# Two MLPs behind linear attention: converted weights kept in DRAM as split parts, and the leaky ReLU moved into ScalarE's pass over the bank

## The chip, the core and the metric

One core of one Trainium2 chip runs the whole program. The time is that of the device for one execution, in microseconds, the median of several runs. TensorE multiplies, VectorE and ScalarE work on tiles element by element, GpSimd does next to nothing here, and SyncE issues all DMA transfers, in order, from one queue.

## The reference

Linear attention with exponential features over 4 batches, 8 heads, 576 tokens of 64 values, then two MLPs over the 2304 tokens of 512 values. The inputs are float64 where the weights are concerned; the result is float32.

```python
def phi(x):
    proj = einsum('bhsd,df->bhsf', x, w_phi)
    proj = proj - max(abs(proj), axis=-1, keepdims=True)
    return concatenate([exp(proj), exp(-proj)], axis=-1)
...
num = einsum('bhsf,bhfd->bhsd', q_p, kv);  den = einsum('bhsf,bhf->bhs', q_p, z)[..., None] + 1e-06
x = num / den                        # [2304, 512]
h = x @ w_in                         # 512 -> 2048
x = maximum(0.01 * h, h) @ w_out     # 2048 -> 512
g = x @ w_gate                       # 512 -> 1536
out = (g / (1 + exp(-g)) * (x @ w_val)) @ w_out2
```

## The kernel before

The program goes batch by batch. The attention of batch 0 runs alone at the start; then come the two MLPs of batch 0, with the attention of batch 1 spread between their units, and so on to the MLPs of the last batch, which run alone.

A *unit* is 24 matmuls: 12 products for each half of the batch's 576 tokens (288 columns), each half in a PSUM bank of its own (`products`, L523 to L533). A hidden tile of 128 features takes one unit in the first MLP (`u_l1`) and two in the second (`u_gate`, `u_val`); 4 hidden tiles are then multiplied by the second weights in 4 units of `u_out`. Each float32 factor is held as a high part in float32r and a low part that is the rest, and a product is made of three matmuls: high by high, high by low, low by high. So a weight tile of 128 x 512 is used as a tile of 128 x 2 x 512, which `w_split` makes: ScalarE copies the high part (L510) and VectorE subtracts it from the whole (`sub`, L57).

The weights come as float64. In batch 0 each tile is loaded as such (`w_load`, L477, 512 KB), turned into float32 by two passes of ScalarE (L491, L492) and three of VectorE (L493 to L499) in `w_to_f32`, and stored as float32 to DRAM (`kept`, L504, 256 KB). Batches 1 to 3 load that copy (L480) and split it again. Eight gate weights are converted in the first attention already (`early`).

The pools hold five buffers for float64 tiles and split tiles of the first weights (`wi`), four for split tiles of the second weights (`wo`), four for float32 weights (`wr`). A tile pool gives a buffer when its last reader is done, so a load can wait for TensorE, VectorE or ScalarE, or for a store. `splits` writes loads ahead by up to five weights, conversions by two. The order on each engine is then laid out once, when the program is built, by a scheduler that goes by priorities and its own estimate of durations; on the chip each engine works through its list in order.

The leaky ReLU stands in `u_l1`. ScalarE copies each half out of its bank into `es` (through `cp`, L60), VectorE then makes max(0.01 g, g) in place over both halves (L554), and `to_parts` splits the result into `gp`:

```python
for c, ps in products(in_ops(("1", b, f), xh, xl, b)):
    cp(g[:, c], ps)
dve.scalar_tensor_tensor(out=g, in0=g, scalar=0.01, in1=g, op0=ALU.mult, op1=ALU.max)
to_parts(g, ("1", b, f))
```

## Time and profile before

| what | value |
|---|---|
| runs | 1099.57, 1102.17 and 1103.4 us, median 1102.17 |
| profiled execution, first to last instruction (span) | 1099.4 us |
| TensorE busy | 1078.7 us (98%), 7728 matmuls |
| VectorE busy | 854.7 us (78%) |
| ScalarE busy | 659.9 us (60%) |
| moved by DMA | 130.25 MB, mean 118 GB/s |

The profile is of one execution; its span lies 2.8 us under the median of the runs. Busy is the time in which at least one instruction of the engine runs. Matmuls are pipelined, so that each lasts about 295 ns while one starts every 133 ns; a gap between two starts shows as idle only as far as it is longer than a matmul lasts.

### The profile page before, as it was taken

How to read it: one execution, taken by the hardware profiler on the slowest of the kernel's cores; microseconds unless marked ns; L12 is line 12 of the kernel's file. 1: busy time of each engine (PE TensorE's matmuls, PEld its weight loads, DVE VectorE, ACT ScalarE, POOL GpSimd, SP SyncE). 2: the span in 40 equal slices, each digit the busy share in tenths (PEclk: the TensorE clock that was granted, in tenths of full speed). 3: DMA queues.
4: the chain of work that ended last, by engine and by line, in shares of the span. 5: the costliest groups of instructions: out<-in, count | busy, mean ns of one | idle time of the engine just before them, and what ended most of it. 6: DMA issues, size and time to landing. Idle time of an engine off the chain costs nothing.

```text
span 1099.4 us, 20402 instructions
## 1 busy us (share of the span) xinstructions
PE 1078.7 (98%) x7728; PEld 1041.9 (95%) x7728; DVE 854.7 (78%) x1765; ACT 659.9 (60%) x1457; POOL 6.8 (1%) x28
## 2 busy tenths in 40 slices
PE   7899999999999999999999999999999999999998
PEld 6668999999998999999999999999999999999998
DVE  6998889898999888779778888878787645565553
ACT  7768877667766787556646576655563444344421
POOL 1000000000000000000000000000000000000000
PEclk9999999999999999999999999999999999999999
DMA  9735766454654532223223322232131232323211
GB/s 332 237 93 174 213 209 194 154 155 155 211 185 125 172 100 91 80 57 110 62 76 108 103 73 89 77 98 97 36 97 51 80 99 77 92 82 106 97 48 44
DMA packets 69329, 130.25 MB, mean 118 GB/s; under 512 B 17136, under 2 KB 17392, under 8 KB 69232
## 3 DMA queue, kind: packets, MB, share of 16 engines
q1 hardware_dynamic: 69232, 128.95, 37.8%
q8 instruction: 61, 1.00, 0.4%
q14 instruction: 36, 0.29, 0.1%
HBM read 106.38 MB, written 22.54 MB: 117 GB/s over the span
## 4 chain that ended last, share of the span: by engine, by line
PE 82%; DVE 5%; DMA 5%; ACT 5%; issue 1%; SPq 0%; ACTq 0%; DVEq 0%
PE pm L530 70%; PE pa L391 4%; DMA wi<-in_w_dram 3%; PE pa L200 3%; PE pa L159 2%; DVE wr L499 1%; DMA wi<-in_wv_dram 1%; DVE wr L494 1%; ACT wr L491 1%; PE pm L299 1%; PE pa L344 1%; ACT wi L492 1%; PE pa L365 1%; PE pa L334 0%; PE pa L335 0%
## 5 line engine op out<-in xcount | busy, mean ns | idle before, releaser
L530 PE MATMUL pm<-xh,wi 128*128 128x288 f32 x2560 | 534.0, 297 | 2.2 <-ACT wi L510 1.6
L530 PEld LDWEIGHTS pm<-xh,wi 128*128 128x128 f32 x2560 | 416.5, 188 | 6.1 <-ACT wi L510 1.8
L530 PE MATMUL pm<-gp,wo 128*128 128x288 f32 x2688 | 385.3, 296 | 2.6 <-ACT acc L60 1.5
L530 PE MATMUL pm<-xl,wi 128*128 128x288 f32 x1280 | 378.9, 297 | 0.0
L530 PEld LDWEIGHTS pm<-gp,wo 128*128 128x128 f32 x2688 | 365.3, 188 | 6.6 <-ACT acc L60 1.8
L530 PEld LDWEIGHTS pm<-xl,wi 128*128 128x128 f32 x1280 | 240.4, 188 | 2.5 <-issue 1.7
L510 ACT ACTIVATE wi<-wr 128x512 fp32r<-128x512 f32 x160 | 101.0, 635 | 59.9 <-PE pm L530 34.6
L57 DVE TENSOR_TENSOR wi<-wr,wi 128x512 fp32r<-128x512 f32 x160 | 108.9, 682 | 14.2 <-ACT wi L510 13.0
L588 DVE TENSOR_TENSOR acc<-pm,acc 128x288 f32<-128x288 f32 x160 | 70.8, 453 | 57.1 <-PE pm L530 56.2
L510 ACT ACTIVATE wo<-wr 128x512 fp32r<-128x512 f32 x112 | 67.2, 630 | 65.5 <-PE pm L530 59.5
L57 DVE TENSOR_TENSOR wo<-wr,wo 128x512 fp32r<-128x512 f32 x112 | 74.3, 682 | 31.0 <-ACT wo L510 30.8
L57 DVE TENSOR_TENSOR gp<-es,gp 128x576 fp32r<-128x576 f32 x112 | 83.8, 749 | 13.5 <-ACT gp L60 12.6
L60 ACT ACTIVATE gp<-es 128x576 fp32r<-128x576 f32 x112 | 76.7, 687 | 25.0 <-DVE es L554 15.6
L561 ACT ACTIVATE es<-pm 128x288 f32<-128x288 f32 x96 | 39.4, 413 | 45.1 <-PE pm L530 44.5
L60 ACT ACTIVATE es<-pm 128x288 f32<-128x288 f32 x128 | 52.5, 417 | 16.5 <-PE pm L530 16.0
L57 DVE TENSOR_TENSOR fl<-ff,fh 128x512 fp32r<-128x512 f32 (+1 forms) x72 | 51.0, 714 | 13.0 <-ACT fh L60 12.7
L569 DVE SCALAR_TENSOR_TENSOR es<-pm,es 128x288 f32<-128x288 f32 x96 | 43.0, 450 | 23.0 <-PE pm L530 22.7
L492 ACT ACTIVATE wi<-wi 128x512 int32<-128x512 uint32 x60 | 41.2, 687 | 32.7 <-DMA wi<-in_w_dram 20.2
L562 DVE SCALAR_TENSOR_TENSOR es<-es,pm 128x288 f32<-128x288 f32 x96 | 42.1, 444 | 20.5 <-ACT es L561 19.9
L554 DVE SCALAR_TENSOR_TENSOR es<-es 128x576 f32<-128x576 f32 x64 | 48.0, 751 | 8.7 <-ACT es L60 8.7
L491 ACT ACTIVATE wr<-wi 128x512 f32<-128x512 f32 x60 | 40.7, 684 | 15.8 <-DMA wi<-in_w_dram 4.7
L394 ACT ACTIVATE dn<-pa 64x288 f32<-64x288 f32 x64 | 26.1, 408 | 37.8 <-PE pa L391 36.8
(108 smaller groups left out, 1282.1 us busy)
## 6 DMA issues: line engine op xcount, KB each, us to landing
wr<-kept SPq DMA_DIRECT2D x212, 256.0 KB, 2.8
wi<-in_w_dram SPq DMA_DIRECT2D x44, 512.0 KB, 4.3
kept<-wr SPq DMA_DIRECT2D x68, 256.0 KB, 4.1
wi<-in_wv_dram SPq DMA_DIRECT2D x12, 512.0 KB, 4.1
raw<-in_kT_dram SPq DMA_DIRECT2D x16, 288.0 KB, 3.1
raw<-in_qT_dram SPq DMA_DIRECT2D x16, 288.0 KB, 3.1
out_dram<-acc SPq DMA_DIRECT2D x16, 288.0 KB, 2.4
gp<-in_wg_dram SPq DMA_DIRECT2D x8, 512.0 KB, 7.8
```

The lines of the kernel that those rows point to most:

```text
L57: dve.tensor_tensor(out=o, in0=a, in1=b, op=ALU.subtract)
L60: act.activation(o, a, AF.Copy)
L391: pe.matmul(ps, w, x, start=(i == 0), stop=(i == len(ops) - 1))
L491: act.activation(t, high.bitcast(F32), AF.Abs, scale=REBIAS)
L492: act.activation(low, low.bitcast(U32), AF.Copy, scale=2.0**-29)
L510: i = act.activation(t[:, 0], r, AF.Copy)
L530: m = pe.matmul(ps, w, x[:, c], start=(i == 0), stop=(i == n - 1))
L554: dve.scalar_tensor_tensor(out=g, in0=g, scalar=0.01, in1=g, op0=ALU.mult, op1=ALU.max)
L561: act.activation(t[:, c], ps, AF.Tanh, scale=0.5)
L562: dve.scalar_tensor_tensor(out=t[:, c], in0=t[:, c], scalar=1.0, in1=ps, op0=ALU.add, op1=ALU.mult)
L569: dve.scalar_tensor_tensor(out=g[:, c], in0=ps, scalar=0.5, in1=g[:, c], op0=ALU.mult, op1=ALU.mult)
L588: dve.tensor_tensor(out=acc[o][:, t], in0=ps, in1=acc[o][:, t], op=ALU.add)
```

## The change

Weights are split once. `w_split` now ends by storing both parts to DRAM in one transfer of 512 KB, and batches 1 to 3 load the parts straight into the tile that TensorE reads. The store of the float32 form goes, but for the eight gate weights of `early`, which keep it (`ready`). `wo` has five buffers in place of four, `wr` three in place of four. In `u_l1` ScalarE makes the leaky ReLU (Prelu with slope 0.01) as it empties the bank, and VectorE's pass goes. That each half has a bank of its own is so before as well.

```diff
-    kept = {}
+    kept, ready = {}, {}
+    def parts_tile(key):
+        wtile[key] = t = T([P, 2, 512], F32R, *(("wo", 5) if key[0] in "23" else ("wi", 5)))
+        return t
+    def flat(t):
+        return t.rearrange("p a n -> p (a n)").bitcast(F32)
+    def keep(cols, src_ap):
+        uid[0] += 1
+        d = dram.tile([P, cols], F32, name=f"kept_{uid[0]}")
+        nc.sync.dma_start(out=d, in_=src_ap)
+        return d
     def w_load(key, tag="wi", n=5):
-        kind, b, f = key
-        if b == 0 and (kind, f) not in kept:
+        kind, _, f = key
+        if (kind, f) in kept:
+            nc.sync.dma_start(out=flat(parts_tile(key)), in_=kept[kind, f])
+        elif (kind, f) in ready:
+            wf[key] = t = T([P, 512], F32, "wr", 3)
+            nc.sync.dma_start(out=t, in_=ready[kind, f])
+        else:
             w64[key] = t = T([P, 512, 2], I32, tag, n)
             nc.sync.dma_start(out=t.rearrange("p n t -> p (n t)"), in_=src[kind][f].bitcast(I32))
-        else:
-            wf[key] = t = T([P, 512], F32, "wr", 4)
-            nc.sync.dma_start(out=t, in_=kept[kind, f])
 ...
-        t = T([P, 512], F32, "wr", 4)
+        t = T([P, 512], F32, "wr", 3)
 ...
         wf[key] = t
-        kind, _, f = key
-        uid[0] += 1
-        kept[kind, f] = d = dram.tile([P, 512], F32, name=f"kept_{uid[0]}")
-        nc.sync.dma_start(out=d, in_=t)
     def w_split(key):
-        kind, b, f = key
+        if key not in wf:
+            return
         r = wf.pop(key)
-        wtile[key] = t = T([P, 2, 512], F32R, *(("wo", 4) if kind in "23" else ("wi", 5)))
+        t = parts_tile(key)
         i = act.activation(t[:, 0], r, AF.Copy)
         tc.stamp_issue_order_token(i.ins, "weights")
         sub(t[:, 1], r, t[:, 0].bitcast(F32))
+        kept[key[0], key[2]] = keep(1024, flat(t))
     def early(key):
         w_load(key, "gp", 5)
         w_to_f32(key)
-        del wf[key]
+        ready[key[0], key[2]] = keep(512, wf.pop(key))
 ...
         for c, ps in products(in_ops(("1", b, f), xh, xl, b)):
-            cp(g[:, c], ps)
-        dve.scalar_tensor_tensor(out=g, in0=g, scalar=0.01, in1=g, op0=ALU.mult, op1=ALU.max)
+            act.activation(g[:, c], ps, AF.Prelu, alpha=0.01)
         to_parts(g, ("1", b, f))
```

The scheduler lays out the whole list anew. The first place is ScalarE's list around the first unit of batch 0. L510 (now L523) is the copy of a weight's high part; `wi_68_294` (now `wi_66_290`) is the fourth weight of the first MLP and `wo_284_945` (now `wo_282_940`) the first of its second product; `es` is the output of a unit. Before:

```order
L492 ACTIVATE wi_65_284<-wi_65_284 128x512 [waits DMAHW2_49]
L510 ACTIVATE wi_68_294<-wr_62_273 128x512 [waits DVE_49,Activation_49]
L510 ACTIVATE wo_284_945<-wr_66_286 128x512
L394 ACTIVATE dn_227_758<-pa_226_755 64x288 [waits PE_49]
L394 ACTIVATE dn_227_758<-pa_231_770 64x288 [waits PE_49]
L491 ACTIVATE wr_298_1007<-wi_65_284 128x512 [waits DVE_49]
L60 ACTIVATE xh_222_745<-xf_221_742 128x288 [waits DVE_49]
L373 ACTIVATE ff_252_831<-pa_251_828 128x288 [waits PE_49]
```

And of the change:

```order
L508 ACTIVATE wi_64_282<-wi_64_282 128x512 [waits DMAHW2_49,Activation_49]
L170 ACTIVATE ff_332_1148<-pa_330_1144,mn_333_1149 128x128 [waits DVE_49,PE_49,Activation_49]
L171 ACTIVATE ff_332_1148<-pa_330_1144,mk_331_1146 128x128
L170 ACTIVATE ff_332_1148<-pa_330_1144,mn_333_1149 128x128
L171 ACTIVATE ff_332_1148<-pa_330_1144,mk_331_1146 128x128
L523 ACTIVATE wi_66_290<-wr_61_271 128x512 [waits PE_49]
L567 ACTIVATE es_277_902<-pm_279_917 128x288
L523 ACTIVATE wo_282_940<-wr_65_284 128x512
L170 ACTIVATE ff_340_1193<-pa_338_1189,mn_341_1194 128x128 [waits DVE_49,Activation_49]
L171 ACTIVATE ff_340_1193<-pa_338_1189,mk_339_1191 128x128
L567 ACTIVATE es_293_971<-pm_295_986 128x288 [waits PE_49]
```

Before, both copies stand among the last steps of the first attention (L394, L373), ahead of every unit's output; now they stand among the keys of the next attention (L170, L171) and the outputs of the first units (L567), and the first of them waits for TensorE.

The second place is VectorE's list a little later, at the outputs of the first units: L554 is the leaky ReLU, L57 with `wi`, `wo` or `gp` a subtraction that makes a low part, L164 and L168 belong to the next attention. Before:

```order
L554 SCALAR_TENSOR_TENSOR es_278_904<-es_278_904 128x576 [waits Activation_49]
L57 TENSOR_TENSOR wi_288_958<-wr_282_937,wi_288_958 128x512 [waits PE_49,Activation_49]
L57 TENSOR_TENSOR wo_300_1015<-wr_286_950,wo_300_1015 128x512 [waits Activation_49]
L57 TENSOR_TENSOR wo_312_1072<-wr_298_1007,wo_312_1072 128x512 [waits Activation_49]
L164 TENSOR_REDUCE mk_351_1253<-pa_350_1251 128x2 [waits PE_49]
L57 TENSOR_TENSOR wo_329_1143<-wr_310_1064,wo_329_1143 128x512 [waits Activation_49]
L554 SCALAR_TENSOR_TENSOR es_294_974<-es_294_974 128x576 [waits Activation_49]
L554 SCALAR_TENSOR_TENSOR es_306_1031<-es_306_1031 128x576 [waits Activation_49]
```

And of the change:

```order
L57 TENSOR_TENSOR wi_66_290<-wr_61_271,wi_66_290 128x512 [waits Activation_49]
L57 TENSOR_TENSOR wo_282_940<-wr_65_284,wo_282_940 128x512 [waits Activation_49]
L164 TENSOR_REDUCE mk_350_1246<-pa_349_1244 128x2 [waits PE_49]
L168 TENSOR_SCALAR mn_352_1249<-mk_350_1246 128x2 [waits DVE_49]
L164 TENSOR_REDUCE mk_361_1301<-pa_360_1299 128x2 [waits PE_49,Activation_49]
L168 TENSOR_SCALAR mn_363_1304<-mk_361_1301 128x2 [waits DVE_49]
L57 TENSOR_TENSOR gp_280_931<-es_277_902,gp_280_931 128x576 [waits Activation_49]
L509 TENSOR_SCALAR wr_285_947<-wr_285_947 128x512 [waits Activation_49]
L509 TENSOR_SCALAR wr_297_1003<-wr_297_1003 128x512 [waits Activation_49]
```

The three passes of L554 are gone. Where the low parts of the fifth weight and of the second, third and fourth `wo` tile stood, now the fourth weight and the first `wo` tile are made, and conversions (L509) stand behind them.

The third place is SyncE's list in the second batch, where kept weights are loaded. Before:

```order
L480 DMA wr_1365_6413<-kept_710_3046 128x512 [waits DMAHW4_49,DVE_49]
L480 DMA wr_1381_6483<-kept_729_3147 128x512 [waits DMAHW6_49,DVE_49]
L480 DMA wr_1383_6488<-kept_230_768 128x512 [waits DMAHW7_49,DVE_49]
L480 DMA wr_1388_6524<-kept_754_3282 128x512 [waits DMAHW0_49,DVE_49]
L480 DMA wr_1405_6596<-kept_243_806 128x512 [waits DMAHW5_49,DMAHW1_49,DVE_49]
```

And of the change:

```order
L490 DMA wi_1012_4603<-kept_358_1293 128x1024 [waits DMAHW2_49,PE_49]
L490 DMA wi_1023_4659<-kept_369_1348 128x1024 [waits DMAHW3_49,PE_49]
L490 DMA wi_1049_4778<-kept_390_1430 128x1024 [waits DMAHW4_49,PE_49]
L490 DMA wi_1098_5028<-kept_452_1724 128x1024 [waits DMAHW5_49,PE_49]
L130 DMA raw_1324_6209<-in_qT_dram 128x576 [waits DMAHW6_49,DVE_49]
L490 DMA wo_1064_4864<-kept_404_1495 128x1024 [waits DMAHW7_49,PE_49]
```

A load waited for VectorE, which had to split the tile that was in its `wr` buffer; now it waits for TensorE, which has to be done with the tile in its `wi` or `wo` buffer.

## Rows read from the trace of the kernel before

**Rows 1.** The page: span, and busy time of each engine with its instructions

```profile
span 1099.4 us, 20402 instructions
PE 1078.7 (98%) x7728; PEld 1041.9 (95%) x7728; DVE 854.7 (78%) x1765; ACT 659.9 (60%) x1457; POOL 6.8 (1%) x28
```

**Rows 2.** By stages: us, busy PE, PEld, DVE, ACT, POOL (instructions), clock, DMA share, GB/s

```profile
0.00:87.00 87.00, 74.83 (x328) 57.59 (x328) 73.40 (x187) 62.44 (x144) 4.88 (x21) 1.00 0.67 220
87.00:220.00 133.00, 131.66 (x903) 126.02 (x904) 116.75 (x239) 104.59 (x249) 1.87 (x7) 1.00 0.61 188
220.00:345.00 125.00, 121.25 (x852) 115.23 (x851) 116.27 (x254) 84.69 (x173) 0.00 (x0) 1.00 0.56 176
345.00:603.00 258.00, 257.98 (x1939) 254.03 (x1938) 213.42 (x441) 166.32 (x385) 0.00 (x0) 1.00 0.31 94
603.00:860.00 257.00, 257.00 (x1937) 253.49 (x1935) 210.69 (x425) 154.39 (x332) 0.00 (x0) 1.00 0.27 80
860.00:1099.40 239.40, 235.94 (x1778) 235.54 (x1776) 124.12 (x223) 87.44 (x176) 0.00 (x0) 1.00 0.26 80
```

**Rows 3.** The chain that ended last, its last long piece: start us, us, what

```profile
862.81 233.15 PE pm L530 x1756
```

**Rows 4.** Waits of PE, 87 to 345 us: us in total, times, longest

```profile
PE pm L530 <- ACT wi L510: 1.6, 1, 1.6
PE pm L530 <- ACT acc L60: 1.5, 1, 1.5
```

**Rows 5.** The timeline, 258 to 264 us: start, us, engine, instruction, idle before

```profile
261.25 0.67 ACT L492 ACTIVATE wi<-wi 128x512 int32<-128x512 uint32 x1 [0.70 <-DMA wi<-in_wv_dram]
...
262.41 1.85 PE L530 MATMUL pm<-gp,wo 128*128 128x288 f32 x12 [1.51 <-ACT acc L60]
```

**Rows 6.** Waits of ScalarE for float64 loads, 87 to 345 us

```profile
ACT wi L492 <- DMA wi<-in_w_dram: 20.2, 15, 2.6
ACT wi L492 <- DMA wi<-in_wv_dram: 10.5, 8, 2.0
```

**Rows 7.** Groups by line: busy us, mean ns of one, idle before and its releasers

```profile
L57 DVE TENSOR_TENSOR wi<-wr,wi 128x512 fp32r<-128x512 f32 x160 | 108.9, 682 | 14.2 <-ACT wi L510 13.0
L510 ACT ACTIVATE wi<-wr 128x512 fp32r<-128x512 f32 x160 | 101.0, 635 | 59.9 <-PE pm L530 34.6 <-DMA wr<-kept 11.3 <-issue 10.2
...
L57 DVE TENSOR_TENSOR wo<-wr,wo 128x512 fp32r<-128x512 f32 x112 | 74.3, 682 | 31.0 <-ACT wo L510 30.8
...
L510 ACT ACTIVATE wo<-wr 128x512 fp32r<-128x512 f32 x112 | 67.2, 630 | 65.5 <-PE pm L530 59.5 <-DMA wr<-kept 4.4 <-DVE wr L499 1.4
L60 ACT ACTIVATE es<-pm 128x288 f32<-128x288 f32 x128 | 52.5, 417 | 16.5 <-PE pm L530 16.0
...
L554 DVE SCALAR_TENSOR_TENSOR es<-es 128x576 f32<-128x576 f32 x64 | 48.0, 751 | 8.7 <-ACT es L60 8.7
...
L561 ACT ACTIVATE es<-pm 128x288 f32<-128x288 f32 x96 | 39.4, 413 | 45.1 <-PE pm L530 44.5
...
L175 ACT ACT_TABLE_LOAD x1 | 1.3, 1283 | 0.7 <-PEq L758 0.7
```

**Rows 8.** Line L554 alone, 87 to 220 us: us, VectorE busy (instructions)

```profile
87.00:220.00 133.00, 11.93 (x16) 1.00 0.61 188
```

**Rows 9.** DMA: queue 1, and transfers with KB each and median us to landing

```profile
q1 hardware_dynamic: 69232, 128.95, 37.8%
...
wr<-kept SPq DMA_DIRECT2D x212, 256.0 KB, 2.8
wi<-in_w_dram SPq DMA_DIRECT2D x44, 512.0 KB, 4.3
kept<-wr SPq DMA_DIRECT2D x68, 256.0 KB, 4.1
```

**Rows 10.** Groups by line: conversions of weights

```profile
L499 DVE TENSOR_TENSOR wr<-wr,wi 128x512 uint16<-128x512 uint16 x60 | 44.8, 751 | 0.2
...
L492 ACT ACTIVATE wi<-wi 128x512 int32<-128x512 uint32 x60 | 41.2, 687 | 32.7 <-DMA wi<-in_w_dram 20.2 <-DMA wi<-in_wv_dram 10.5 <-DMA wi<-in_wg_dram 1.7
```

## The prediction

> **What bounds the kernel now.** I read the busy times first: TensorE is busy 1078.7 of 1099.4 us, VectorE 854.7, ScalarE 659.9 [rows 1]. With an engine at 98%, what other engines save can only shorten the 20.7 us in which it is not busy, so the next view is the one by stages, where the reader is to see where these lie [rows 2]. The columns give: 12.2 us idle before 87 us (first attention, start-up loads), 1.3 from 87 to 220 (first batch, first MLP), 3.8 from 220 to 345 (first batch, second MLP), 0.02 from 345 to 860 (the second and third batch), and 3.5 behind 860 us, most of it the last result's way out. The chain of waits ends in one piece of 1756 matmuls in 233.15 us [rows 3]: 132.8 ns each. In the last three batches TensorE runs at that pace without a gap that this view shows, and VectorE (83% from 345 to 860 us) and ScalarE (60 to 64%) keep ahead of it. The granted clock is 1.00, the higher level of 2.4 GHz, in every stage [rows 2], so no term stands for it.
>
> So the reader should look at the first batch, 87 to 345 us, alone. There all weights are converted from float64, and VectorE is at 88 and 93% [rows 2]. The waits of TensorE in that stretch name two large ones: 1.6 us for a weight copy by ScalarE and 1.5 us for an evacuation into acc by ScalarE [rows 4]. In both cases ScalarE was late for the same reason: its queue is in order, and a conversion that waits for a float64 tile stands in front. The row at 261.25 us shows it: the conversion had waited 0.70 us for its load, and behind it comes the evacuation that TensorE waits 1.51 us for [rows 5]. ScalarE waits for such loads 20.2 + 10.5 us in this stretch [rows 6].
>
> **The change part by part.**
>
> *Splits in the later batches.* 204 weight tiles (68 in each of three batches) are no longer split: ScalarE loses 204 x 0.63 = 129 us, VectorE 204 x 0.68 = 139 us [rows 7]. All of it lies beside matmuls, in stages whose TensorE idle time is 0.02 us. Gain on the path: 0, since this view leaves 0.02 us to win there. The two splits of a tile also leave the way of a weight from its load to its use, which makes the later batches safer, not faster.
>
> *Leaky ReLU.* The copy out of the bank costs 417 ns, the Tanh with the same shape 413 [rows 7]: on this engine the function does not set the price, so I take 417 for Prelu (bounds 413 and, were it two passes, 834: 128 x 417 = 53 us more of ScalarE over the run, hidden except in 87 to 220 us, where 32 of them are 13 us). VectorE loses 64 passes of 0.75 us, 48 us; 11.93 us of that in 87 to 220 us [rows 7, 8]. The Trainium skill's page ScalarE: Activation LUTs, section Rules for kernel authors, says to put relu and max on VectorE rather than ScalarE. By that rule the move would be a loss. The row says otherwise here, because the ScalarE pass over the bank is there already: 417 ns stay 417 ns, and 751 ns go. What the move can win is the 1.3 us of TensorE idle time in 87 to 220 us [rows 2], from a VectorE queue that is shorter by 9% there. I take 1.3.
>
> *Second MLP of the first batch.* No leaky ReLU lies here, and the conversions and splits of this batch's own weights stay. Only the splits for the next batch's first tiles go at its end. The 3.8 us come from ScalarE waiting for loads, which is not removed. I take a gain of 0.5 (0 to 2).
>
> *Loads and stores.* A reload was 256 KB and landed in 2.8 us; it becomes 512 KB, for which the float64 loads of the same size say 4.3 us [rows 9]. 204 x 0.262 MB = 53 MB more are read; 68 stores double and 8 early ones are added, 76 x 0.262 = 20 MB more. Queue 1 moved 128.95 MB in 37.8% of the engines' time [rows 9], so 202 MB are about 59% (an estimate in proportion). In the later batches 94 GB/s become about 163 at a share of 0.31, so about 0.54: room remains, and the buffers are asked for several units ahead. The first batch is tighter: its share is 0.61 and 0.56 at 188 and 176 GB/s [rows 2]; 20 MB over 258 us are 77 GB/s more, a share near 0.83. A float64 load then takes longer than 4.3 us, and ScalarE's queue stands for that time. Price: from 0 (it hides under the lead of the loads) to the 23 waits for loads [rows 6] being 0.5 us longer each, of which two large ones reach TensorE now and four may: +2. I take +0.5.
>
> *Order in the first batch.* This is the part the diff does not tell. The program as built splits the fourth weight of the first MLP behind a wait for TensorE, where before it was done ahead of the first unit; the first weight of the second product comes behind it too. A split is 0.63 us on ScalarE and then 0.68 on VectorE [rows 7], which are ten matmuls at 132.8 ns. Counted in the built order, eleven of the first batch's 68 weights now have their last split step released by a matmul that lies under 15 places ahead of their first use; before there were two. One converted buffer fewer (wr 4 to 3) and split tiles that are held for their store make this lead shorter. Where the lead is shorter than the split, TensorE waits for the rest: 0 to 1.3 us each, up to the 1.6 us of the one case that the trace has [rows 4]. Some of the eleven lie next to each other and share one wait, and the low part is asked for a few matmuls behind the high one, so I take four waits of 0.5: +2. Bounds 0 and six times 1.6.
>
> *Start-up.* Before the first unit's output ScalarE has seven instructions fewer (conversions at 0.69 and copies at 0.63 us), and VectorE the passes that belong to them, the longest 0.75 us [rows 7, 10]. The 12.2 us before 87 us are mostly first loads; I take a gain of 1.2 (0 to 3).
>
> **The sum.** -1.3 - 0.5 + 0.5 + 2 - 1.2 = -0.5 us on the profiled 1099.4 us: 1098.9. The runs have a median of 1102.17, 2.8 us above that span, so the time is about 1101.7 us.
>
> **The rivals.** *Gaps close (faster).* The freed VectorE time lets conversions run ahead, and all 5.1 us of 87 to 345 us go, with some 2 us of the start: 1102.2 - 7 = 1095 us. For it: VectorE at 88 and 93% is the fullest engine behind TensorE there. Against it: the two largest waits are ScalarE's, and behind loads.
>
> *Weights late in the first batch (slower).* The place is the first group of the second product and the second MLP's weights in the first batch: splits released by the matmuls just before. Six such waits of 1 to 1.6 us are +6 to +10, with nothing won: 1108 us. It decides from four waits on. For it: the shorter leads, the fuller DMA queue. Against it: the list was ordered with these leads known, and the units in between can fill.
>
> *Reloads late in the later batches (slower).* The 512 KB come too late after all. 204 loads with 0.1 us of wait each are 20 us: 1122 us. Against it: loads are released four or more units, over 12 us, ahead.
>
> *Table loads (slower).* Prelu would need another table than Exp and Tanh, which stand between the units. One load is 1.28 us [rows 7]; two for each of 64 units are 164 us, 41 of them in 87 to 220 us, where ScalarE has 28 us free: at least 13 us, 1115 us. The built program has a single table load, as before, so this has next to no chance. The same page (section Table sets) lists relu, copy and abs as in every set, but not Prelu by name, and no run here shows it yet.
>
> **How the numbers follow.** Little changes: 0.42, 1101.7 us, own range 1098 to 1106. Gaps close: 0.30, 1092 to 1098. Weights late: 0.25, 1106 to 1112. Reloads late 0.02, tables 0.01. What a measurement of this kernel can tell from no change is about 0.3%, 3.3 us, so 1098.9 to 1105.5 counts as the same. Faster 0.30, same 0.42, slower 0.28. The range 1092 to 1111 leaves out the two small rivals and the ends of the others, 2 in 10 at most.
>
> **What would show it.** Right: TensorE's idle time stays between 15 and 22 us, all of it before 345 us; the later batches keep their 258 and 257 us; Prelu takes 0.41 to 0.43 us; VectorE is near 667 us, ScalarE near 531, 204 MB are moved. Wrong on the first batch: TensorE waits for copies into wi or wo of over 6 us in 87 to 345 us (slower), or none of over 1 us and ScalarE's waits for loads under 20 us (faster). Wrong on the later batches: waits of TensorE for kept tiles. Wrong on the start: the first unit begins more than 3 us earlier or later.

## The result, and the profile after

The changed kernel takes 1114.53 us (median of 4 runs, 1112.89 to 1115.18) beside 1102.5 us for the kernel before: ratio 1.011, 95% interval 1.0095 to 1.0125. That is 12 us slower, and 3.5 us above the range of the prediction.

The page shows the work gone as forecast, and TensorE, which has the same 7728 matmuls, busy for longer and idle for longer than in [rows 1]: 28.7 us of the span against 20.7.

```profile
span 1113.3 us, 19800 instructions
PE 1084.6 (97%) x7728; PEld 1046.2 (94%) x7728; DVE 705.0 (63%) x1497; ACT 561.5 (50%) x1253; POOL 6.7 (1%) x28
...
q1 hardware_dynamic: 70384, 202.35, 52.6%
...
L567 ACT ACTIVATE es<-pm 128x288 f32<-128x288 f32 x128 | 52.9, 416 | 107.5 <-PE pm L544 107.0
...
wi<-kept SPq DMA_DIRECT2D x120, 512.0 KB, 3.3
wo<-kept SPq DMA_DIRECT2D x84, 512.0 KB, 5.2
wi<-in_w_dram SPq DMA_DIRECT2D x44, 512.0 KB, 5.1
kept<-wi SPq DMA_DIRECT2D x40, 512.0 KB, 4.2
```

Prelu out of the bank (L567) takes 416 ns where the copy took 417 [rows 7]; a reload of parts lands in 3.3 to 5.2 us, a float64 load in 5.1 in place of 4.3 [rows 9]. VectorE has 150 us less to do and ScalarE 98, and none of it came back as time.

The view by stages answers [rows 2], with the same columns and bounds:

```profile
0.00:87.00 87.00, 76.24 (x324) 59.88 (x324) 68.15 (x173) 57.78 (x136) 4.75 (x21) 0.96 0.60 199
87.00:220.00 133.00, 129.28 (x870) 121.39 (x871) 108.54 (x225) 105.44 (x249) 1.92 (x7) 1.00 0.74 256
220.00:345.00 125.00, 116.90 (x805) 110.71 (x805) 114.06 (x245) 81.98 (x167) 0.00 (x0) 0.99 0.69 234
345.00:603.00 258.00, 255.37 (x1916) 250.99 (x1915) 170.46 (x364) 136.36 (x321) 0.00 (x0) 1.00 0.50 175
603.00:860.00 257.00, 257.00 (x1937) 253.67 (x1937) 165.46 (x342) 122.41 (x266) 0.00 (x0) 1.00 0.42 148
860.00:1113.30 253.30, 249.83 (x1884) 249.56 (x1882) 78.32 (x151) 57.56 (x116) 0.00 (x0) 1.00 0.45 158
```

The reader should look at two columns. TensorE's count of matmuls is 4 lower ahead of 87 us, 33 lower from 87 to 220, 47 lower from 220 to 345 and 23 lower from 345 to 603 us: 107 in all, about 14.2 us at 132.8 ns each, of work that had to follow later; the span is 13.9 us longer. The last 23 are lost by 380 us (the lines below, from 87 to 380 us, before and then after, differ by 105; a matmul across the edge of two windows counts in both), so the loss lies in the first batch and where it passes into the second. The granted clock, 1.00 everywhere before, is 0.96 ahead of 87 us and 0.99 from 220 to 345 us. From 380 us on TensorE is busy up to the last result's way out (3.5 us idle behind 860 us, as before): the loads of 512 KB harm nothing there.

```profile
87.00:380.00 293.00, 287.89 (x2017) 275.79 (x2018) 265.81 (x561) 215.86 (x489) 1.87 (x7) 1.00 0.58 179
```

```profile
87.00:380.00 293.00, 278.55 (x1912) 263.42 (x1913) 254.58 (x540) 211.88 (x477) 1.92 (x7) 0.99 0.72 250
```

What TensorE waits for from 220 to 380 us is neither the weights of [rows 4] nor the accumulator. It is steps of the next batch's attention (L334, L365, L391):

```profile
PE pa L334 <- ACT ff L374: 4.0, 2, 3.4
PE pa L365 <- DVE mrow L354: 2.4, 1, 2.4
PE pa L391 <- DVE xf L409: 1.8, 1, 1.8
PE pm L544 <- DVE es L575: 1.1, 1, 1.1
PE pm L544 <- DVE wi L57: 0.7, 1, 0.7
PE pa L200 <- DVE fl L57: 0.4, 1, 0.4
PE pm L544 <- ACT wi L523: 0.3, 1, 0.3
```

The largest of them in the timeline (start, us, engine, instruction, idle before):

```profile
304.06 0.29 PE L544 MATMUL pm<-xl,wi 128*128 128x288 f32 x1
...
305.87 0.67 ACT L508 ACTIVATE wi<-wi 128x512 int32<-128x512 uint32 x1 [2.07 <-DMA wi<-in_w_dram]
...
306.55 0.41 ACT L394 ACTIVATE dn<-pa 64x288 f32<-64x288 f32 x1
306.97 0.41 ACT L373 ACTIVATE ff<-pa 128x288 f32<-128x288 f32 x1
...
307.27 0.40 ACT L374 ACTIVATE ff<-pa 128x288 f32<-128x288 f32 x1
...
307.73 0.40 PE L334 MATMUL pa<-pk,wst_h 128*128 128x288 f32 x1 [3.37 <-ACT ff L374]
```

ScalarE stands 2.07 us at a conversion whose float64 tile has not landed; three attention steps stand behind it in its queue; TensorE waits 3.37 us for the last of them. This is the shape of [rows 5], with an attention step in the place of the accumulator. Ahead of the two next largest waits ScalarE has stood in the same way, and steps of VectorE stand between it and TensorE:

```profile
243.87 0.70 ACT L508 ACTIVATE wi<-wi 128x512 int32<-128x512 uint32 x1 [1.43 <-DMA wi<-in_wv_dram]
...
246.75 0.53 PE L365 MATMUL pa<-mrow,sel 128*128 128x288 f32 x2 [2.38 <-DVE mrow L354]
...
321.85 0.67 ACT L508 ACTIVATE wi<-wi 128x512 int32<-128x512 uint32 x1 [2.57 <-DMA wi<-in_wg_dram]
...
324.27 1.94 PE L391 MATMUL pa<-ff,kvh 128*128 128x288 f32 x7 [1.77 <-DVE xf L409]
```

The first attention looks worse too. Windows of ten us there, before, then after:

```profile
20.00:30.00 10.00, 9.52 (x47) 8.09 (x45) 8.02 (x19) 9.90 (x26) 1.03 (x4) 1.00 1.08 387
30.00:40.00 10.00, 9.10 (x40) 6.51 (x39) 9.83 (x25) 9.07 (x22) 0.98 (x3) 1.00 0.85 253
```

```profile
20.00:30.00 10.00, 8.13 (x38) 6.20 (x37) 8.42 (x19) 9.91 (x25) 1.04 (x4) 0.98 1.07 387
30.00:40.00 10.00, 9.82 (x32) 7.86 (x33) 8.00 (x20) 6.66 (x16) 0.63 (x2) 0.68 0.76 240
```

and what stands there in the timeline after:

```profile
26.52 0.67 ACT L507 ACTIVATE wr<-wi 128x512 f32<-128x512 f32 x1
...
27.08 0.67 ACT L508 ACTIVATE wi<-wi 128x512 int32<-128x512 uint32 x1
...
27.64 0.42 ACT L176 ACTIVATE ff<-ff 128x256 f32<-128x256 f32 x1
...
27.94 0.63 ACT L523 ACTIVATE wi<-wr 128x512 fp32r<-128x512 f32 x1
...
28.15 1.10 PE L200 MATMUL pa<-ff,pk 96*128 96x256 f32 x4 [1.13 <-issue]
...
28.46 0.68 ACT L508 ACTIVATE wi<-wi 128x512 int32<-128x512 uint32 x1
...
29.03 0.42 ACT L175 ACTIVATE ff<-ff 128x256 f32<-128x256 f32 x1
...
29.48 0.42 ACT L176 ACTIVATE ff<-ff 128x256 f32<-128x256 f32 x1
...
29.95 2.08 PE L200 MATMUL pa<-ff,pk 96*128 96x256 f32 x4 [0.69 <-ACT ff L176]
...
31.82 3.62 PE L159 MATMUL pm<-wbd,raw 128*128 128x256 f32 x8
```

Conversions and splits of the first MLP's weights (L507, L508, L523) stand ahead of the attention's L175 and L176. TensorE stands idle for 1.13 us (till just behind the end of an L176), then for 0.69 us; before, the same two gaps were 0.48 and 0.18 us. Behind that the granted clock is 0.68 from 30 to 40 us, a mean between the two levels of 2.4 and 1.2 GHz, and 32 matmuls start there in place of 40.

Yet little of it is left a few steps later. By 70 us both kernels have started 249 matmuls, the first unit begins at 68.20 us where it began at 67.77, and by 87 us the count is 324 against 328, about 0.5 us. So the crowded start is plain to see and is not where the 12 us went.

### The profile page after: what moved, and what is told of

Read it like the earlier page. It is cut to its first block, busy times and chain, and to the rows that moved or that the text cites. A ratio compares the mean times of both kernels' runs of the same rounds, so it can differ in the third digit from the quotient of the medians.

```text
span 1113.3 us, 19800 instructions
## 1 busy us (share of the span) xinstructions
PE 1084.6 (97%) x7728; PEld 1046.2 (94%) x7728; DVE 705.0 (63%) x1497; ACT 561.5 (50%) x1253; POOL 6.7 (1%) x28
## 3 DMA queue, kind: packets, MB, share of 16 engines
q1 hardware_dynamic: 70384, 202.35, 52.6%
## 4 chain that ended last, share of the span: by engine, by line
PE 86%; DMA 5%; ACT 4%; DVE 3%; issue 1%; SPq 0%; ACTq 0%; DVEq 0%
PE pm L544 73%; PE pa L391 4%; PE pa L200 4%; DMA wi<-in_w_dram 3%; PE pa L159 2%; DMA wi<-in_wv_dram 1%; PE pm L299 1%; ACT wi L508 1%; DMA kept<-wi 1%; PE pa L334 1%; PE pa L344 1%; PE pa L238 1%; PE pa L365 1%; PE pa L335 1%; DVE wr L515 0%
## 5 line engine op out<-in xcount | busy, mean ns | idle before, releaser
L544 PE MATMUL pm<-gp,wo 128*128 128x288 f32 x2688 | 390.0, 296 | 0.2 <-DVE acc L601 0.2
L57 DVE TENSOR_TENSOR gp<-es,gp 128x576 fp32r<-128x576 f32 x112 | 84.4, 754 | 98.8 <-ACT gp L60 98.4
L567 ACT ACTIVATE es<-pm 128x288 f32<-128x288 f32 x128 | 52.9, 416 | 107.5 <-PE pm L544 107.0
L57 DVE TENSOR_TENSOR fl<-ff,fh 128x512 fp32r<-128x512 f32 (+1 forms) x72 | 51.4, 716 | 18.5 <-ACT fh L60 17.5
L508 ACT ACTIVATE wi<-wi 128x512 int32<-128x512 uint32 x60 | 41.2, 687 | 28.5 <-DMA wi<-in_w_dram 17.2
L200 PE MATMUL pa<-ff,pk 128*128 128x256 f32 (+1 forms) x160 | 44.5, 395 | 4.4 <-issue 3.4
L60 ACT ACTIVATE fh<-ff 128x512 fp32r<-128x512 f32 (+1 forms) x72 | 47.6, 664 | 0.9
L394 ACT ACTIVATE dn<-pa 64x288 f32<-64x288 f32 x64 | 26.1, 407 | 40.8 <-PE pa L391 39.7
L515 DVE TENSOR_TENSOR wr<-wr,wi 128x512 uint16<-128x512 uint16 x60 | 44.6, 751 | 0.6
L507 ACT ACTIVATE wr<-wi 128x512 f32<-128x512 f32 x60 | 39.8, 683 | 8.2 <-DMA wi<-in_w_dram 3.8
L60 ACT ACTIVATE acc<-pm 128x288 f32<-128x288 f32 x64 | 26.1, 422 | 33.4 <-PE pm L544 33.0
L510 DVE SCALAR_TENSOR_TENSOR wr<-wi,wr 128x512 int32<-128x512 int32 x60 | 40.9, 686 | 0.8
```

The source lines that it names most:

```text
L57: dve.tensor_tensor(out=o, in0=a, in1=b, op=ALU.subtract)
L60: act.activation(o, a, AF.Copy)
L200: pe.matmul(ps[:, 256 * h : 256 * h + 256], v[:n, h].rearrange("p a d -> p (a d)"), part[b, j, s][:n, h].rearrange("p a f -> p (a f)"), st ...
L508: act.activation(low, low.bitcast(U32), AF.Copy, scale=2.0**-29)
L510: dve.scalar_tensor_tensor(out=ti, in0=high, scalar=-0x80000000, in1=ti, op0=ALU.bitwise_and, op1=ALU.bitwise_or)
L515: dve.tensor_tensor(out=t16, in0=t16, in1=e16, op=ALU.add)
```

## The experiments

Three theories: **the ring** (three buffers for converted weights in place of four), **the stores** (512 KB of parts for each weight in the first batch, which also hold the split tile), **the order** (any edit makes the scheduler draw a new order, and this one is bad). The price of the order can't be removed, only drawn again. Ratios are to the kernel before on the same chip, with their 95% intervals; the kernel before has medians of 1101.65 to 1103.04 us on these chips, so a difference of two times from different chips is good to about 1.4 us.

**Each half of the change alone.** The first edit is the leaky ReLU alone, the second the stored parts alone:

```diff
--- before.py, Prelu alone
-            cp(g[:, c], ps)
-        dve.scalar_tensor_tensor(out=g, in0=g, scalar=0.01, in1=g, op0=ALU.mult, op1=ALU.max)
+            act.activation(g[:, c], ps, AF.Prelu, alpha=0.01)
--- after.py, parts alone
-            act.activation(g[:, c], ps, AF.Prelu, alpha=0.01)
+            cp(g[:, c], ps)
+        dve.scalar_tensor_tensor(out=g, in0=g, scalar=0.01, in1=g, op0=ALU.mult, op1=ALU.max)
```

> The kernel before with the leaky ReLU alone moved to ScalarE (Prelu); weights are stored as float32 and split in every batch as before. If what was lost comes from the smaller ring of converted weights (theory one) or from the doubled stores and the tiles that they hold (theory two), neither is here: 1098 to 1103 us, no clock row under 0.95 and no wait of TensorE over 2.5 us between 87 and 380 us. If it comes from any new order that the list scheduler makes, whatever the edit (theory three), the time can lie anywhere from 1095 to 1112 us.

> The changed kernel with the leaky ReLU put back: a Copy out of the bank by ScalarE, then a pass over both halves by VectorE. Theories one and two: the loss stays, 1112 to 1118 us, waits of TensorE for attention steps (the lines 334, 365, 391) between 220 and 345 us of over 5 us in all. Theory three: anywhere from 1098 to 1118 us. If Prelu itself were the harm, 1099 to 1103 us.

Measured: Prelu alone 1102.72 us, 1.0002 (0.9992 to 1.0013): no change. Parts alone 1118.91 us, 1.0159 (1.0134 to 1.0185). The loss belongs to the stored parts and the rings that were set with them. That parts alone is 4.4 us slower than the whole change says nothing of Prelu: a redraw, below, moves as much. And the mark that I gave did not come: TensorE does not wait for attention steps there but for weights, as these largest waits from 87 to 380 us show (L200 belongs to the attention):

```profile
PE pm L544 <- ACT wi L523: 9.2, 7, 2.5
PE pa L200 <- issue: 2.3, 3, 1.8
PE pm L544 <- DVE wi L57: 1.8, 2, 1.6
PE pm L544 <- ACT wo L523: 1.1, 1, 1.1
```

**Four buffers, a single store, and both.**

```diff
--- after.py, four buffers
-            wf[key] = t = T([P, 512], F32, "wr", 3)
+            wf[key] = t = T([P, 512], F32, "wr", 4)
...
-        t = T([P, 512], F32, "wr", 3)
+        t = T([P, 512], F32, "wr", 4)
--- after.py, a single store
-        kept[key[0], key[2]] = keep(1024, flat(t))
+        if not kept:
+            one.append(keep(1024, flat(t)))
+        kept[key[0], key[2]] = one[0]
```

> The changed kernel with four buffers for converted weights again in place of three; nothing else. Theory one (the ring of three): ScalarE's waits for a converted buffer to come free (on the subtraction of line 57) go, and the time falls to 1099 to 1105 us. Theory two (stores): 1111 to 1116 us. Theory three: some other time between 1098 and 1118 us, and the waits lie in other places.

> The changed kernel with a single store: the parts of the first split weight are stored, and all later batches load these same 512 KB in place of their own weight, so the later batches compute with a wrong weight; what is left out is 67 of the 68 stores of parts (35 MB) and the wait of a tile for its store. Theory two: 1098 to 1104 us, the DMA share from 87 to 345 us falls from 0.72 to near 0.5, and float64 loads land in about 4.3 us in place of 5.1. Theory one: 1111 to 1116 us. Theory three: any other time between 1098 and 1118 us.

> The changed kernel with a single store of parts (later batches load these 512 KB in place of their own weight and so compute with a wrong one) and four buffers for converted weights. Each of the two alone left most of the loss (1113.8 and 1111.2 us). If the smaller ring and the stores do the harm together, each able to do it alone, this is 1098 to 1104 us. If the new order of the instructions does it, the time stays over 1106 us, with waits of TensorE for attention steps between 220 and 380 us, although neither the ring nor the stores are left to blame.

Measured: four buffers 1111.15 us, 1.0082 (1.0065 to 1.0099); a single store 1113.76, 1.0105 (1.0089 to 1.0122); both 1101.8, 0.9993 (0.9982 to 1.0003). With three buffers the stores cost nothing that can be told (1114.53 against 1113.76), although the DMA share from 87 to 380 us falls from 0.72 to 0.42 without them: the bytes are not the cause there. The windows, first of four buffers, then of four buffers and a single store, show what the ring does from 87 to 380 us; the changed kernel has 278.55 us and 1912 matmuls there.

```profile
30.00:40.00 10.00, 8.77 (x25) 6.93 (x26) 8.41 (x20) 6.14 (x15) 0.63 (x2) 0.66 0.94 276
87.00:380.00 293.00, 287.27 (x1972) 273.78 (x1971) 248.23 (x529) 208.75 (x472) 1.88 (x7) 0.99 0.71 247
```

```profile
30.00:40.00 10.00, 8.74 (x27) 6.95 (x28) 8.81 (x22) 6.50 (x16) 0.63 (x2) 0.68 0.67 197
87.00:380.00 293.00, 289.56 (x2030) 277.81 (x2029) 250.45 (x536) 211.12 (x482) 1.88 (x7) 1.00 0.45 143
```

The fourth buffer gives TensorE 9 us and 60 matmuls in that stretch, yet the time falls by 3.4 us only: the start is worse in this kernel than in the changed one, TensorE is busy for 40.3 us from 40 to 87 us in place of 43.5, and 297 matmuls start ahead of 87 us in place of 324. The clock row from 30 to 40 us is low in both lines, 0.66 and 0.68, and the second kernel takes no longer than the kernel before: a low row there is not by itself a loss. One mark of the ring theory failed: ScalarE's waits at L507 for VectorE to free a buffer (L57) did not go (3.7 us from 87 to 380 us with three buffers, 1.9 + 1.8 by its two rows, and 3.1 with four).

**An extra buffer in the kernel before, and both kernels under another scheduler.**

```diff
--- before.py
-        wtile[key] = t = T([P, 2, 512], F32R, *(("wo", 4) if kind in "23" else ("wi", 5)))
+        wtile[key] = t = T([P, 2, 512], F32R, *(("wo", 5) if kind in "23" else ("wi", 5)))
--- before.py and after.py
-    with _tile.TileContext(nc, schedule_with_timeline_sim=True) as tc:
+    with _tile.TileContext(nc, schedule_with_timeline_sim=False) as tc:
```

> The kernel before with one more buffer for the split weights of the second products (five in place of four), and nothing else: more room, no work. If the loss is physical (ring, stores, transfers), this is 1097 to 1103 us. If the order that the scheduler makes decides, a changed ring gives another order, and the time can lie anywhere from 1095 to 1115 us.

> The kernel before, with its instructions ordered by priority alone in place of by the scheduler's own model of time. It serves as the other half of the next run: a second pair of before and after under another order. The time itself is open, 1100 to 1250 us.

> The changed kernel, ordered by priority alone as in the run ahead of it. If the harm is physical (shorter ring, stores that hold tiles), it is slower than that run by 8 us or more. If the harm is one draw of the scheduler, the difference of the two has no reason to be of that sign: between -15 and +15 us, and faster if the work that VectorE and ScalarE lose counts.

Measured: the extra buffer 1104.3 us, 1.0018 (1.0008 to 1.0028). Ordered by priority, before 1126.68 and after 1118.57: there the same change makes the kernel 8 us faster. TensorE is busy for 284.1 and 279.9 of the 293 us from 87 to 380 us, but it starts 1903 and 1923 matmuls there at a granted clock of 0.98 and 0.99, so by its work the changed kernel leads in that stretch too, as it does up to 87 us (311 and 327) and after 380 us (5281 and 5314 up to 1090 us). The sign of the whole change thus hangs on the order.

**The stores on another queue; the first conversions later.**

```diff
--- after.py with four buffers, stores from GpSimd's queue
-        nc.sync.dma_start(out=d, in_=src_ap)
+        (eng or nc.sync).dma_start(out=d, in_=src_ap)
...
-        kept[key[0], key[2]] = keep(1024, flat(t))
+        kept[key[0], key[2]] = keep(1024, flat(t), nc.gpsimd)
--- after.py with four buffers, first weights at a lower priority
         if i == 8:
-            splits(-1)
+            with tc.high_priority(offset=-200):
+                splits(-1)
```

> The changed kernel with four buffers for converted weights, and the stores of the parts issued from GpSimd's queue in place of SyncE's. With four buffers the stores still cost 1111.2 - 1101.8 = 9 us. If they cost it because the loads of float64 weights and of the attention's inputs stand behind them in SyncE's queue, which waits for each split (39 us of its waiting from 220 to 380 us), this is 1101 to 1105 us. If they cost it by their bytes or by holding the split tile until they have landed, it stays at 1109 to 1113 us.

> The changed kernel with four buffers for converted weights, and the loads, conversions and splits of the first weights, which run beside the first attention, put at a lower priority there. If the conversions that stand ahead of attention steps in ScalarE's queue near 28 us make the gap after which the granted clock is 0.66 to 0.68 from 30 to 40 us, the clock row there returns to 1.00 and the time falls by 3 to 6 us, to 1105 to 1108 us. If the loads of the attention's inputs make that gap, or the weights now come late for the first unit, no gain: 1109 to 1114 us.

Measured: the other queue 1108.64 us, 1.0051 (1.0032 to 1.007), between the two forecasts: about 2.5 us less than four buffers alone. The later conversions 1102.97 us, 1.0007 (0.9991 to 1.0023): 8.2 us less than four buffers alone, more than forecast, and the clock row is back:

```profile
30.00:40.00 10.00, 8.87 (x43) 6.92 (x42) 9.97 (x24) 8.76 (x21) 1.15 (x4) 1.00 0.84 244
87.00:380.00 293.00, 286.97 (x2000) 274.93 (x2001) 247.87 (x527) 208.75 (x475) 1.87 (x7) 0.99 0.74 254
```

**Parts stored a batch later.** The first batch is that of the kernel before with Prelu; the parts are stored in the second batch and loaded from the third on. The second of the two runs adds the lower priority of the first weights.

```diff
--- before.py with Prelu and five buffers "wo"
+        if (kind, f) in parts:
+            nc.sync.dma_start(out=t.rearrange("p a n -> p (a n)").bitcast(F32), in_=parts[kind, f])
...
         sub(t[:, 1], r, t[:, 0].bitcast(F32))
+        if b == 1:
+            parts[kind, f] = d = dram.tile([P, 1024], F32, name=f"parts_{uid[0]}")
+            nc.sync.dma_start(out=d, in_=t.rearrange("p a n -> p (a n)").bitcast(F32))
```

> Leaky ReLU by ScalarE; in the first batch float32 weights are stored at their conversion as in the kernel before (four buffers for them); in the second batch they are loaded and split again, and the parts stored there; the third and fourth batch load the parts. Five buffers for the split weights of the second products. If the loss of the change comes from the smaller ring and the stores of parts in the crowded first batch, nothing of it is here: 1097 to 1103 us. If any new order costs as much, it can be 1095 to 1113 us, with waits of TensorE in the first batch.

> The kernel of the run ahead of it (parts stored in the second batch), with the first weights' loads, conversions and splits at a lower priority beside the first attention. If conversions ahead of attention steps cost time there in every order, 2 to 4 us less than that run. If not, equal within 2 us, or slower by the first unit's wait for its weights.

Measured: 1107.83 us, 1.0056 (1.0034 to 1.0079), and 1115.39, 1.0119 (1.0103 to 1.0136). Both miss. The first does the work of Prelu alone in the first batch, yet TensorE is busy for 281.0 us from 87 to 380 us in place of 287.3 and starts 74 matmuls fewer. Of these 50 are lost by 345 us, while the first store of parts is issued at 351 us. Neither a ring of three nor stores of parts stand there, so the order is left as the cause; the fifth buffer, the other difference, alone cost 0.2% above. In the second the lower priority harms: its start was not crowded (clock 1.00 from 30 to 40 us without it), and TensorE's busy time from 40 to 87 us falls from 42.17 to 38.20 us.

**Three buffers with the mended start, and redraws.** A redraw changes one number of the scheduler's priorities, and no work:

```diff
-                with tc.high_priority(offset=50):
+                with tc.high_priority(offset=60):
```

> The changed kernel (three buffers for converted weights) with the loads, conversions and splits of the first weights at a lower priority beside the first attention. If the ring of three and the crowded start are two separate causes, the start gains about 3 us (no clock row under 0.95 before 100 us) and the waits of TensorE from 87 to 380 us stay at 10 us or more: 1108 to 1113 us. If the start alone was the cause, 1100 to 1105 us.

> The changed kernel, with the attention steps of the later batches at a priority offset of 60 in place of 50: no work, buffer or transfer changes, only the order. If the ring of three is a cause in any order, 1108 to 1120 us with waits of TensorE of 10 us or more from 87 to 380 us. If the order is the whole cause, it may be anywhere from 1099 to 1120 us, and the waits may be under 7 us.

> The mended kernel (four buffers, first conversions at a lower priority: 1103.0 us), redrawn in the same way. If the two mends remove causes, 1099 to 1108 us. If its time was a lucky draw, 1108 to 1118 us.

> The kernel before, redrawn in the same way. It says how far an order alone moves a kernel that has neither the ring of three nor the stores of parts: 1097 to 1110 us; if it stays within 3 us of 1102, an order alone is a small cause, and if it rises to 1108 or more, a large one.

Measured: three buffers with the lower priority of the first weights (the *mended start*) 1108.93 us, 1.0053 (1.0038 to 1.0068), in the range that the two-cause theory gave. The *mended kernel* has four buffers as well. The windows of the first:

```profile
30.00:40.00 10.00, 9.45 (x45) 7.56 (x44) 9.77 (x25) 8.27 (x21) 1.15 (x5) 1.00 0.74 235
87.00:380.00 293.00, 280.56 (x1923) 266.55 (x1922) 251.76 (x532) 208.72 (x466) 1.91 (x7) 0.98 0.74 254
```

Of the 47 matmuls that it has started more than the changed kernel by 380 us, 36 lie ahead of 87 us, where the changed kernel was only 4 behind the kernel before. So the mended start is mostly a new gain, not a loss undone.

The redraws: changed kernel 1119.25 us, 1.0143 (1.0126 to 1.0159); mended kernel 1107.63, 1.0047 (1.003 to 1.0063); kernel before 1101.86, 0.999 (0.998 to 1.0001). A redraw moves the two with stored parts by 4.7 us each and the kernel before by less than can be told. Within either order the two mends together are worth the same: 1114.53 - 1102.97 = 11.6 us, and 1119.25 - 1107.63 = 11.6 us. In both nearly all of it lies from 87 to 380 us: 88 and 93 matmuls more there, and 10 and 2 more ahead of 87 us.

**The stores once ring and start are mended.** The mended kernel with the single store of above, and with the stores on GpSimd's queue as above.

> The mended kernel (four buffers, first conversions at a lower priority) with a single store of parts, which all later batches load in place of their own weight, so that they compute with a wrong one. If the stores cost what they did with the crowded start, it is 5 to 9 us under the mended kernel's 1103.0 and 1107.6 us: 1095 to 1100 us. If that was a draw, 1101 to 1107 us.

> The mended kernel with the stores of parts issued from GpSimd's queue. Of the mends that the runs so far point to, these three are additive if they remove separate waits: 1103.0 - 2.5 = 1100.5 us, below both kernels by 2 us or more at best. If the queue was not a cause and its 2.5 us a draw, 1101 to 1108 us.

Measured: 1101.35 us, 0.9986 (0.9976 to 0.9996), and 1101.3, 0.9986 (0.9968 to 1.0004). The stores cost 1.6 us here, about what an interval spans; the 9 us that they seemed to cost beside a crowded start were not shown to be theirs. By stages the single store gives 28 matmuls more from 87 to 380 us, 3.7 us, and has 23 fewer ahead of 87 us; a redraw of the mended kernel moves 28 there as well, so a cost of the stores of that size is neither shown nor excluded. The last kernel beats the changed one by 1.2%, but not the kernel before by more than its interval tells.

TensorE's busy time and matmuls in the 293 us from 87 to 380 us, by the view of windows, put the runs side by side:

| kernels | busy us | matmuls |
|---|---|---|
| three buffers, parts stored: changed, parts alone, redraw, other scheduler, single store, mended start | 276.3 to 280.6 | 1878 to 1923 |
| four buffers, parts stored: alone, other queue, mended, redraw of mended, mended with other queue | 285.0 to 288.4 | 1971 to 2018 |
| four buffers, a single store, with either start | 289.2 and 289.6 | 2028 and 2030 |
| float32 stored in the first batch: before, Prelu alone, extra buffer, redraw | 286.1 to 287.9 | 1987 to 2017 |
| the same, before under the other scheduler | 284.1 | 1903 |
| the same, parts stored a batch later, with either start | 281.0 and 281.4 | 1935 and 1921 |

Where each kernel falls behind is seen when the matmuls ahead of 87 us are put beside them:

| kernel | first unit, us | matmuls to 87 us | 87 to 380 us | span, us |
|---|---|---|---|---|
| before | 67.77 | 328 | 2017 | 1099.4 |
| changed | 68.20 | 324 | 1912 | 1113.3 |
| parts alone | 65.89 | 334 | 1878 | 1117.5 |
| changed, redrawn | 66.17 | 332 | 1879 | 1117.7 |
| three buffers, mended start | 63.04 | 360 | 1923 | 1107.3 |
| four buffers | 69.98 | 297 | 1972 | 1109.0 |
| mended: four buffers, mended start | 63.21 | 334 | 2000 | 1100.4 |
| mended, redrawn | 63.22 | 334 | 1972 | 1104.9 |
| four buffers, a single store | 69.15 | 312 | 2030 | 1099.9 |
| the same, mended start | 67.05 | 311 | 2028 | 1100.2 |

In each of these rows the matmuls that are missing by 380 us against the kernel before, at 132.8 ns each, give its longer span to within 0.6 us: for the changed kernel 4 + 105 of them, 14.5 us, where the span is 13.9 us longer. Parts alone and the redraw are even ahead at 87 us and lose the most.

## Why the prediction was wrong

*What held.* The bound was read rightly: nothing that left VectorE and ScalarE in the later batches came back as time, and from 380 us TensorE is busy without a gap up to the last result's way out. (VectorE's share from 345 to 860 us was 82%, not the 83 that I read.) Prelu costs 416 ns, and 202.35 MB go through queue 1, as forecast. VectorE's 705.0 us and ScalarE's 561.5 lie 38 and 31 us above my 667 and 531: I took off the durations of the removed instructions, but instructions that follow each other overlap (in the timeline above L374 begins at 307.27 us, 0.11 us ahead of the end of L373), and busy time counts the overlap once. The reloads are not late.

*The step that failed: "Order in the first batch".* It read "I take four waits of 0.5: +2. Bounds 0 and six times 1.6", and it named "one converted buffer fewer (wr 4 to 3)". The place was right and the term too small: from 87 to 380 us TensorE starts 105 matmuls fewer, 13.9 us, more than the upper bound of 9.6. The fourth buffer gives back 60 of them, and 77 beside the mended start (1923 to 2000). In the time it is worth 3.4 us (1114.53 to 1111.15) and 5.9 us (1108.93 to 1102.97), since either kernel with four buffers has 26 or 27 matmuls fewer ahead of 87 us. My count of short leads looked at weights alone. In the changed kernel TensorE waits for copies into wi for 0.2 us from 87 to 345 us, far from the over 6 us that I gave as the mark of a slower kernel; attention steps behind a late conversion make 8.2 us (4.0 + 2.4 + 1.8). In parts alone, another order with the same ring, the mark is met: 7.4 us for copies into wi and wo in that stretch. Which step waits is a matter of the draw.

*"Leaky ReLU", -1.3, and "Second MLP", -0.5.* These gains were to come from the same stretch, and did not. Prelu alone gave 1.0002 (0.9992 to 1.0013), so nothing. The Trainium skill's page ScalarE: Activation LUTs, section Rules for kernel authors, which would keep it on VectorE, is not borne out as a loss either: the pass on ScalarE was there already, and 64 passes of VectorE were hidden.

*"Start-up".* It read "I take a gain of 1.2 (0 to 3)" from ScalarE having fewer instructions ahead of the first unit. The count was right, and no gain came: the first unit begins 0.43 us later, and 4 matmuls are missing at 87 us, about 0.5 us. Conversions stand earlier in ScalarE's queue, ahead of attention steps, and I had not counted what stands ahead of each of these. Moving the conversions back gave 5.6 us with three buffers (1114.53 to 1108.93) and 8.2 us with four (1111.15 to 1102.97), but 0.5 us with four and a single store (1101.8 to 1101.35), where the clock row had been 0.68 too. So a better start was to be had, and a worse one was not what made the changed kernel slow.

*"Loads and stores", +0.5.* The runs neither bear it out nor refute it: the stores cost 0.8 us with three buffers, 9.4 with four and 1.6 with both mends, and a redraw moves 4.7. The share of the first batch is 0.74 and 0.69, where the estimate had 0.83, and queue 1 takes 52.6%, where it had 59.

*The rivals.* "Weights late in the first batch", at 1108 us and 0.25, was nearest: slower, in that batch, by short leads, with nothing won. The changed kernel has attention steps in the place of its weights, and parts alone has the weights. "Gaps close" failed: VectorE was freed, from 116.75 to 108.54 us in 87 to 220 us, and TensorE idled for longer. That time on the fullest engine behind TensorE buys nothing while ScalarE's queue stands at a load.

*What is shown, and what stays open.* The counts show where the time goes: 105 of 109 matmuls are lost from 87 to 380 us. The edits show the ring as one cause: among kernels that store parts in the first batch, under the same scheduler, the five with three buffers start 1878 to 1923 matmuls there and the seven with four buffers 1971 to 2030. It is not the whole: four buffers alone give back 3.4 of the 12 us, and only with the single store or the mended start, two different edits, is the time that of the kernel before. What these two do, beyond a new order, is not settled. Nor is it settled how three buffers make a step late: ScalarE's own waits for a buffer are no longer with three than with four, and its waits for float64 loads from 87 to 380 us are 30.2 and 30.0 us, so that loads issued later are not seen there. Nor why parts stored a batch later lose as much in a first batch with four buffers. An order alone can cost as much as the ring, as that run shows, and the other scheduler turns the sign of the whole change. So each single time here is good to about 5 us as a statement on its edit, whatever its interval; what was drawn more than once carries the conclusion.

## What to carry to other kernels

Where an engine's queue is in order and two kinds of work share it, count what a change puts ahead of the other kind, and not only ahead of the work that it serves: in the changed kernel the weights came in time and the attention steps behind them did not. An edit that makes the changed kernel faster has not by that undone what made it slow: compare each stage with the kernel before, as the count of matmuls does here. A buffer ring that is cut to pay for another one is a term of the sum with a price of its own, even if the freed engine time is ten times as large. Where a scheduler sets the order, measure an edit under a second draw before the cause is put down to it.

## What the hardware showed unexpectedly

TensorE's granted clock fell behind short gaps, and not in every case. In the changed kernel TensorE was busy for 8.13 of the 10 us from 20 to 30 us and the row behind is 0.68, in which eight matmuls of 256 columns took 3.62 us (at 31.82 us); in the redraw of the changed kernel it was busy for 8.16 of them and the row behind is 1.00. With 10.00 of 10 us (the mended start, with three and with four buffers) it stayed at 1.00. The low row cost the changed kernel little: by 70 us it has started as many matmuls as the kernel before. Stores of 512 KB issued by GpSimd kept that engine busy, 35.56 us from 87 to 380 us where it had 1.88, and cost TensorE nothing that the runs show.
